# Loads of keys, values and weights in pieces of 1 to 1.5 KB, and a longer hand-written list for the first part

## The chip, the core and the metric

The kernel runs on one core of one Trainium2 chip. A core has a matrix engine (TensorE, PE in the profile, with the weight loads apart as PEld), three engines for elementwise work (VectorE or DVE, ScalarE or ACT, GpSimd or POOL), an engine that issues transfers (SyncE or SP) and 16 DMA engines that move data between the device memory and the on-chip memory. The metric is device time in microseconds, the median of several runs. What is looked at in the profile is one execution.

## What is computed

Four batches of 768 tokens go through three steps, all in fp32:

```python
# 1: attention, 4 x 8 heads of 64, in chunks of 32 tokens: each chunk sees 8 memory keys,
#    16 keys to its left, its own 32 and 8 to its right
scores = scale * q_c @ k_full.T
a = exp(scores - max); a = a / (sum(a) + 1e-09)
x = a @ v_full
# 2: mixing over tokens
theta = x @ w_theta
y = w_tok_r @ (x * cos(theta)) + w_tok_i @ (x * sin(theta))
u = x + y
x = u + relu(u @ w_ch)
# 3: a gated MLP with a token mix
h = gelu(x @ w_in); u, v = halves of h
out = x + (u * (w_sg @ layernorm(v) + b_sg)) @ w_out
```

## The kernel before, in words

**Arithmetic.** Products run on TensorE at reduced precision, so each operand is split into a high and a low part, and three matmuls (high x high, high x low, low x high) stand for one. Weights are split once (`conv_*`, for `w_theta` and `w_tok`), operands as they come (`op_hi` on ACT, `op_lo` on DVE).

**Stages.** The attention goes through 24 blocks of 128 tokens, six for each batch. Behind each block stand theta's matmuls (four steps of three). The token mix of batch 0 runs as plain products between the blocks (`mix_pe`), 48 of them. The token mix of batches 1 to 3 runs as Strassen-Winograd: seven products on half-size operands, each in two halves of 18 matmuls of 128 x 384 (`prod`, L593 to L614, the matmul is L611). For it the weights are combined into s1, s2, s3, a22 (`t_raw`, `t_hi`, `t_lo`, for i = 1 to 4; the combination t3, which makes s3, is used by product 5, and its raw result lies in the room `rin`). x and the fractions of theta of these batches are stored to device memory (`store_xt`, `store_ft`) and loaded again (`in_load`), for batches 2 and 3 into three rooms in `rin`. From them come the operands a11 to a22: sine and cosine on ACT (`zz_sin`, `zz_abs`, `zz_cos`), times x on DVE (`zz_mul`). Then come relu(u @ w_ch) (`chan`) and the MLP, which the change leaves alone.

**What sets the order.** The first part is written out by hand: the string `OPENING` is a list of words, and inside `tc.manual_schedule()` each engine gets its instructions in the list's order, each issued by the function that the table `step` names. Behind the list, from L1104 on, Python code is written in natural order and a scheduler places it. Before, the list ends with `P.1.3.1`, the second half of product 3 of batch 1, and the rest of batch 1 (operand 4, t3, products 4 to 6, the reload for batch 2) is placed by the scheduler.

**Words that the change and the prediction touch.** `q.i`, `k.i`, `v.i`: loads of block i, with two buffers each, on SP's queue as all transfers are. `wt.k`, `wm.j`: loads of pieces of `w_theta` and `w_tok`. `S.i`: scores, 64 small matmuls and their 64 weight loads (`pairs`, L282 to L293, the matmul is L287); `V.i`: probabilities times values, the same shape; `T`, `X`: transposes (L345, L377). `A.i.k`: theta's matmuls (L412); `ac`, `af`: its fraction, on ACT and DVE (L418, L422). `M.n.g`: token mix of batch 0 (L472). `W.n`: n matmuls on the constant tile `busy` whose result nobody reads (L1071); here they are called fillers. `P.b.j.e`: half e of product j of batch b. `ss`, `oh`, `ol`: the sum, high and low part of an operand (L580, L584, L589). `t3`, `t3h`, `t3l`: the steps of t3 (DVE L506 to L509, ACT L515, DVE L518). `cx`, `cy` and, new, `rd`: the reads of finished products, which add a PSUM bank into a sum on DVE (`o_add`, L633); `lr`/`lo` and `sr`/`rs` load and store these sums. `li.b.d.h.j`: the reload (`in_load`, L537), then `ZS`, `ZA`, `ZC`, `ZZ`.

**Layout of the loads.** A block's k is one transfer of 128 rows, each 4096 B in one piece; v has 4160 B a row, `w_theta` 4096 B, `w_tok` 6144 B. x and theta are stored as 2048 B a row, and batch 1 reads them again as three pieces of 1024 B a row, since it takes half of the columns at a time.

Of the kernel before, what the change touches and what calls it, by code (L numbers as in the profile page):

```python
# [19 lines left out]
DM = H * D  # L20
# [14 lines left out]
wt.0 q.0 q.1 wt.1 id.0 wt.3 k.0 k.1 thH.0 v.0 v.1 thR.0 ths.0 wt.2 thg.0 wm.0 wm.1 tha.0 wm.2 thh.0  # L35
thl.0 thH.1 thR.1 ths.1 thg.1 tha.1 thh.1 W.16 S.0 thl.1 q.2 m.0 thH.3 k.2 p.0 thR.3 ths.3 e.0 W.6
S.1 thg.3 k.3 T.0 m.1 q.3 t.0 p.1 tha.3 e.1 W.3 V.0 thh.3 v.2 r.0 T.1 thH.2 x.0 t.1 ths.2 thR.2 X.0
thg.2 w.0 tha.2 h.0 thl.3 thh.2 l.0 tkH.1 thl.2 sT.0 W.8 A.0.0 tkR.1 tks.1 A.0.1 tkg.1 tkH.0 A.0.2
tkR.0 tks.0 tkg.0 S.2 m.2 k.4 A.0.3 q.4 p.2 ac.0 tka.0 e.2 V.1 af.0 tkh.0 v.3 T.2 r.1 wm.3 t.2 x.1
tkl.0 X.1 S.3 tka.1 as.0 w.1 q.5 m.3 wm.4 h.1 k.5 p.3 aa.0 l.1 ak.0 W.5 V.2 z.0 sT.1 A.1.0 v.4 r.2  # L40
x.2 e.3 A.1.1 tkh.1 T.3 tkH.2 tkl.1 S.4 t.3 m.4 q.6 A.1.2 zh.0 k.6 tks.2 tkH.3 X.2 p.4 A.1.3 w.2
tks.3 V.3 h.2 zl.0 ac.1 l.2 v.5 M.0.0 e.4 r.3 sT.2 af.1 tkR.3 T.4 x.3 A.2.0 tkg.2 S.5 tkg.3 as.1 t.4
k.7 A.2.1 aa.1 m.5 lu.5.0 X.3 ak.1 q.7 p.5 tkR.2 A.2.2 z.1 w.3 V.4 tka.3 v.6 A.2.3 r.4 tka.2 M.0.1
e.5 x.4 ac.2 wm.5 T.5 h.3 wm.6 af.2 S.6 t.5 l.3 zh.1 q.8 m.6 X.4 tkh.3 sT.3 A.3.0 p.6 k.8 w.4 M.0.2
tkl.3 h.4 e.6 A.3.1 l.4 tkH.5 zl.1 T.6 sT.4 A.3.2 tkh.2 tks.5 V.5 tkl.2 v.7 A.3.3 r.5 as.2 x.5 t.6
M.1.0 tkg.5 ac.3 aa.2 X.5 af.3 ak.2 S.7 w.5 z.2 as.3 q.9 A.4.0 m.7 zh.2 k.9 tkH.6 M.1.1 zl.2 h.5
tks.6 A.4.1 aa.3 p.7 ak.3 M.1.2 tkg.6 z.3 V.6 l.5 e.7 v.8 A.4.2 tkR.5 r.6 sT.5 x.6 T.7 tkR.6 A.4.3
tka.5 t.7 S.8 tka.6 ac.4 tkh.5 q.10 X.6 m.8 k.10 M.0.3 tkh.6 af.4 sx.6 lu.5.1 p.8 w.6 A.5.0 lu.5.2
zh.3 tkl.5 M.1.3 e.8 zl.3 h.6 V.7 l.6 tkl.6 sT.6 T.8 v.9 as.4 A.5.1 r.7 t.8 x.7 aa.4 A.5.2 ak.4
tkH.4 z.4 S.9 zh.4 q.11 m.9 A.5.3 tkR.4 k.11 X.7 p.9 ac.5 zl.4 sx.7 V.8 w.7 af.5 h.7 v.10 r.8 A.6.0  # L50
# [41 lines left out]
def net_kernel(tc, qt, kw, vw, ident, w_theta, w_tok, w_ch, w_in, w_sg, w_out, g_ln, b_sg, out):  # L92
# [225 lines left out]
    def load_k(i):  # L318
        nc.sync.dma_start(out=ka[i % 2], in_=kw[i])

    def load_v(i):
        nc.sync.dma_start(out=va[i % 2], in_=vw[i])
# [270 lines left out]
    def prod(b, j, e):  # L593
# [4 lines left out]
        if j == 1:  # L598
            bank["y", e] = acc_tile()[:, 0:TC]
# [736 lines left out]
```

## Time and profile before

| what | value |
|---|---|
| median of 3 runs | 752.41 us (752.05 to 753.37) |
| profiled execution | 756.5 us, its span 754.4 us |
| mean granted TensorE clock | 0.977 |
| TensorE busy | 709.2 us (94%) |
| VectorE, ScalarE busy | 533.8 us (71%), 376.3 us (50%) |
| transfers | 59,861 packets, 118.32 MB, mean 157 GB/s |
| chain that ended last | PE 73%, DVE 11%, DMA 7%, issue 4%, ACT 4% |

The profile is of one execution, which took 756.5 us; the runs that are timed have no profile. Times in the trace count from the start of the span. "Busy" adds up the instructions of an engine, where matmuls overlap. "Issue" as what ended a wait means that the engine waited for nothing that the profile shows. The granted clock is a share of full speed. In the trace the opening list goes to about 270 us, `P.1.3.1`; the products of batch 1 end at about 297 us; `chan` and the MLP fill the time from 385 us on.

### The profile page before, as it was taken

To read this page: it belongs to the slowest core of one execution; us is meant where nothing else is said; L and a number is where in the kernel's file an instruction comes from. 1 tells how busy PE (TensorE), PEld (TensorE's weight loads), DVE (VectorE), ACT (ScalarE), POOL (GpSimd) and SP (SyncE) were. 2 spreads that over 40 slices of the span, in tenths; PEclk is the share of its full clock that TensorE was granted. 3 is DMA by queue.
4 is the path that set the end of the run, shared out by engine and by line. 5 is a ranking of instruction groups with operands and counts; after the bars stand their busy time and mean duration, and the time that the engine had idled before them with its cause. 6 is when DMAs were issued, how large, how long until landed. Compare 5 with 4: busy or idle time off the path is not lost.

```text
span 754.4 us, 15661 instructions
## 1 busy us (share of the span) xinstructions
PE 709.2 (94%) x6602; PEld 643.2 (85%) x6602; DVE 533.8 (71%) x851; ACT 376.3 (50%) x551; POOL 0.3 (0%) x6
## 2 busy tenths in 40 slices
PE   6789797999899888999999999999999999999997
PEld 3567575787689878999999998999899989998997
DVE  5888697887684995979749955968346744674375
ACT  4889798688663454553516515812251234223320
POOL 0000000000000000000000000000000000000000
PEclk8899899999999988999999999999999999999999
DMA  9888798899664327333439956001300220030002
GB/s 343 302 305 250 256 340 332 265 318 299 215 197 153 124 76 264 111 105 123 147 85 354 310 186 256 3 1 43 125 1 1 88 80 1 1 111 17 0 1 84
DMA packets 59861, 118.32 MB, mean 157 GB/s; under 512 B 5520, under 2 KB 37392, under 8 KB 59792
## 3 DMA queue, kind: packets, MB, share of 16 engines
q1 hardware_dynamic: 59792, 117.33, 46.0%
q8 instruction: 52, 0.85, 0.5%
q14 instruction: 17, 0.14, 0.1%
HBM read 82.71 MB, written 34.60 MB: 156 GB/s over the span
## 4 chain that ended last, share of the span: by engine, by line
PE 73%; DVE 11%; DMA 7%; issue 4%; ACT 4%; SPq 1%; DVEq 0%; ACTq 0%
PE acc L909 13%; PE acc L694 9%; PE acc L802 7%; PE att L611 7%; PE acc L840 7%; PE th L412 6%; PE att L947 6%; PE acc L611 5%; PE acc L472 4%; PE att L287 4%; DMA right<-ft_dram 3%; DMA xT_dram<-left_o 1%; PE th L611 1%; PE att L345 1%; PE th L947 1%
## 5 line engine op out<-in xcount | busy, mean ns | idle before, releaser
L412 PE MATMUL th<-left 128*128 128x512 f32 x288 | 90.2, 425 | 4.0 <-issue 2.1
L611 PE MATMUL att<-left,at 128*128 128x384 f32 x342 | 67.2, 352 | 7.5 <-DVE left_o L633 4.1
L611 PEld LDWEIGHTS att<-left,at 128*128 128x128 f32 x342 | 62.5, 198 | 10.4 <-DVE left_o L633 4.8
L287 PEld LDWEIGHTS att<-at 64*32 64x32 f32 x3072 | 35.6, 110 | 37.1 <-issue 34.7
L694 PE MATMUL acc<-at,in 128*128 128x384 f32 x384 | 66.9, 335 | 0.0
L694 PEld LDWEIGHTS acc<-at,in 128*128 128x128 f32 x384 | 66.6, 188 | 0.0
L909 PE MATMUL acc<-sg_hi,vhi_all 128*128 128x384 f32 x192 | 64.6, 336 | 0.5 <-ACT vhi_all L209 0.5
L909 PE MATMUL acc<-sg_hi,vlo_all 128*128 128x384 f32 x192 | 64.6, 336 | 0.1
L909 PE MATMUL acc<-sg_lo,vhi_all 128*128 128x384 f32 x192 | 64.5, 336 | 0.0
L287 PE MATMUL att<-at 64*32 64x64 f32 (+1 forms) x3072 | 45.2, 234 | 20.0 <-issue 15.2
L412 PEld LDWEIGHTS th<-left 128*128 128x128 f32 x288 | 50.2, 193 | 13.9 <-DVE in L422 3.2
L472 PE MATMUL acc<-left 128*128 128x384 f32 x288 | 59.5, 342 | 1.1 <-issue 1.1
L209 ACT ACTIVATE gop<-gv_all 128x384 fp32r<-128x384 f32 (+1 forms) x28 | 16.0, 571 | 80.6 <-DVE gv_all L918 53.8
L472 PEld LDWEIGHTS acc<-left 128*128 128x128 f32 x288 | 51.0, 188 | 3.9
L584 ACT ACTIVATE at<-right 128x768 fp32r<-128x768 f32 x42 | 34.9, 842 | 37.7 <-DVE right L580 11.8
L914 DVE SCALAR_TENSOR_TENSOR gv_all<-acc,g_col,b_bc 128x384 f32<-128x384 f32 x32 | 19.7, 616 | 43.1 <-PE acc L909 43.1
L611 PE MATMUL acc<-left,at 128*128 128x384 f32 x252 | 44.9, 337 | 0.0
L611 PEld LDWEIGHTS acc<-left,at 128*128 128x128 f32 x252 | 43.8, 188 | 0.3
L840 PE MATMUL acc<-x3lo,in_hi 128*128 128x384 f32 x128 | 43.1, 337 | 0.0
L840 PE MATMUL acc<-x3hi,in_hi 128*128 128x384 f32 x128 | 43.1, 337 | 0.0
L840 PE MATMUL acc<-x3hi,in_lo 128*128 128x384 f32 x128 | 43.1, 337 | 0.0
L589 DVE TENSOR_TENSOR at<-right,at 128x768 fp32r<-128x768 f32 x42 | 39.4, 954 | 5.1 <-ACT at L584 4.6
(188 smaller groups left out, 1468.6 us busy)
## 6 DMA issues: line engine op xcount, KB each, us to landing
at<-vw SPq DMA_DIRECT2D x24, 520.0 KB, 6.0
at<-kw SPq DMA_DIRECT2D x24, 512.0 KB, 6.2
right<-w_tok SPq DMA_DIRECT2D x12, 768.0 KB, 9.0
at<-qt SPq DMA_DIRECT2D x24, 256.0 KB, 5.0
xT_dram<-left_o SPq DMA_DIRECT2D x24, 256.0 KB, 6.6
left_o<-xT_dram SPq DMA_DIRECT2D x32, 192.0 KB, 2.7
u_dram<-left_o SPq DMA_DIRECT2D x32, 192.0 KB, 1.9
right<-u_dram SPq DMA_DIRECT2D x8, 768.0 KB, 5.9
```

What stands on the lines that cost most here:

```text
L287: nc.tensor.matmul(out=out[32 * c:32 * c + 32, j, n * a:n * a + n], lhsT=lhs[h, a, 32 * c:32 * c + 32], rhs=rhs[h, 4 * a + c, :], start=Tr ...
L412: nc.tensor.matmul(out=tmp["th", i], lhsT=a[:, k], rhs=w[:, k], start=(k == 0 and j == 0), stop=(k == KD - 1 and j == 2),)
L472: nc.tensor.matmul(out=acc_t[g][:, 0:TC], lhsT=z_part(n, a)[:, ri, zc], rhs=w_part(s, h, b)[:, ri], start=(first and i == 0), stop=(last a ...
L584: nc.scalar.activation(out=op_room(b, j)[0][:, s], in_=op_src(j, h), func=AF.Copy)
L589: nc.vector.tensor_tensor(out=lo[:, s], in0=op_src(j, h), in1=r32(hi[:, s]), op=ALU.subtract)
L611: nc.tensor.matmul(out=bank[to, e], lhsT=a[:, s, ee], rhs=w[:, s], start=(fresh and i == 0), stop=(i == 3 * NBLK - 1), skip_group_check=no ...
L694: nc.tensor.matmul(out=acc[:, 0:TC], lhsT=w[:, k, ee], rhs=x[:, k, :], start=(i == 0), stop=(i == 3 * KD - 1),)
L802: nc.tensor.matmul(out=acc, lhsT=x[:, k, tt], rhs=w[:, k, :], start=(i == 0), stop=(i == 3 * KD - 1),)
L840: nc.tensor.matmul(out=acc[:, 0:TC], lhsT=w[:, k, ff], rhs=x[:, k, :], start=(i == 0), stop=(i == 3 * KD - 1),)
L909: nc.tensor.matmul(out=acc[:, 0:TC], lhsT=v, rhs=w, start=(i == 0), stop=(i == 3 * NBLK - 1))
L914: nc.vector.scalar_tensor_tensor(out=g, in0=acc[:, 0:TC], scalar=p3["g"][:, f:f + 1], in1=p3["b"][:, tt], op0=ALU.mult, op1=ALU.add,)
L947: nc.tensor.matmul(out=bank, lhsT=wt[:, k, ee], rhs=xt[:, k, :], start=(fresh and i == 0), stop=(i == 5), skip_group_check=not fresh,)
```

## The change

k, v, `w_theta` and `w_tok` are laid out by the host in four pieces a row, so that a row of 128 comes as 4 x 1024 B (v 4 x 1040, `w_tok` 4 x 1536). x and theta are stored as 2 x 1024 B a row, in place of 2048 B, with which batch 1 reads 3072 B in one piece; batches 2 and 3 read 6144 B as before.

The list is a new one and reaches to `P.2.0.1`, the first product of batch 2. It takes in the rest of batch 1: t3, operands 4 to 6, the loads, reads and stores of the sums, the reload for batch 2. `t3` now stands ahead of the operands 4 and 5, right behind `t4l`. Banks are named by batch as well, as batch 2 begins while reads of batch 1 are out. In the list's first part the order of all words is another, and the fillers are 64 matmuls in place of 38.

```diff
 OPENING = """
-wt.0 q.0 q.1 wt.1 id.0 wt.3 k.0 k.1 thH.0 v.0 v.1 thR.0 ths.0 wt.2 thg.0 wm.0 wm.1 tha.0 wm.2 thh.0
...
-cx.1.1 sr.1.0 t4l.0 oh.1.3.0 P.1.2.0 cy.1.1 ss.1.3.1 sr.1.1 ol.1.3.0 oh.1.3.1 ol.1.3.1 P.1.2.1 t4.1
-P.1.3.0 t4h.1 t4l.1 P.1.3.1
+q.0 wt.0 v.0 k.0 q.1 k.1 id.0 wt.1 wt.2 v.1 wt.3 wm.0 wm.1 thH.0 wm.2 ths.0 thR.0 thg.0 tha.0 thh.0
...
+ss.1.4.0 ac.23 ss.1.4.1 t4h.1 af.23 t4h.0 sf.23 P.1.2.0 t4l.1 t4l.0 lo.1.3.0 t3.0 lo.1.2.0 P.1.2.1
+lo.1.1.0 lo.1.2.1 lo.1.3.1 lo.1.1.1 rd.1.2.0 oh.1.4.0 P.1.3.0 t3.1 t3h.0 oh.1.4.1 P.1.3.1 ol.1.4.0
+t3h.1 ol.1.4.1 t3l.1 P.1.4.0 oh.1.5.0 t3l.0 oh.1.5.1 rd.1.2.1 li.2.0.0.0 ol.1.5.1 li.2.0.1.0
...
+P.2.0.0 rd.1.6.1 rs.1.6.1 P.2.0.1
 """
...
-    xt_dram = [dram.tile([128, 3, DM], F32, name=f"xt_dram{i}") for i in range(2 * B)]
-    ft_dram = [dram.tile([128, 3, DM], F32, name=f"ft_dram{i}") for i in range(2 * B)]
+    xt_dram = [dram.tile([128, 2, 3, 256], F32, name=f"xt_dram{i}") for i in range(2 * B)]
+    ft_dram = [dram.tile([128, 2, 3, 256], F32, name=f"ft_dram{i}") for i in range(2 * B)]
...
     def load_k(i):
-        nc.sync.dma_start(out=ka[i % 2], in_=kw[i])
+        nc.sync.dma_start(
+            out=ka[i % 2].rearrange("p (a c) k -> p a c k", a=NPAIR), in_=kw[i].rearrange("a p c k -> p a c k")
+        )
...
-        nc.sync.dma_start(out=xt_dram[c][:, j], in_=xt_t(i))
+        nc.sync.dma_start(out=xt_dram[c][:, :, j], in_=xt_t(i).rearrange("p (d c) -> p d c", d=2))
...
-            nc.sync.dma_start(out=in_src(b, d, h, j), in_=src[:, :, 256 * d:256 * d + 256])
+            nc.sync.dma_start(out=in_src(b, d, h, j), in_=src[:, d])
...
         def load_th(k):
-            nc.sync.dma_start(out=raw_room("th", k), in_=w_theta[k].bitcast(I32))
+            nc.sync.dma_start(
+                out=raw_room("th", k).rearrange("p (g n) -> p g n", g=4),
+                in_=w_theta[k].bitcast(I32).rearrange("g p n -> p g n"),
+            )
...
-        for b in range(1, B):
-            first = 4 if b == 1 else 0
+        for b in range(2, B):
             for r in QUAD:
                 for e in range(2):
...
-                for j in (2, 3):
-                    for e in range(2):
-                        read(b, j, e)
-                operand(b, 4)
-                t_make(3)
-                z_load(2)
-            for j in range(first, 7):
+                    o_load(b, r, e)
+            if b == 2:
+                for e in range(2):
+                    read(b, 0, e)
+                operand(b, 1)
+            for j in range(1 if b == 2 else 0, 7):
```

The order of the transfers on SP at the program's start, before (`in<-w_theta` is `wt`, `at<-qt`, `at<-kw`, `at<-vw` are `q`, `k`, `v`):

```order
L1005 DMA in<-w_theta 128x1024
L316 DMA at<-qt 128x512 x2
L1005 DMA in<-w_theta 128x1024
L997 DMA id_sb<-ident 128x128
L1005 DMA in<-w_theta 128x1024
L319 DMA at<-kw 128x1024 x2
L322 DMA at<-vw 128x1040 x2
```

and after (the line numbers of the changed kernel are up to 14 higher):

```order
L323 DMA at<-qt 128x512
L1016 DMA in<-w_theta 128x4x256
L331 DMA at<-vw 128x4x260
L326 DMA at<-kw 128x4x256
L323 DMA at<-qt 128x512
L326 DMA at<-kw 128x4x256
L1008 DMA id_sb<-ident 128x128
L1016 DMA in<-w_theta 128x4x256 x2
```

The first v and k now stand third and fourth, where the first k was seventh, and three of the four pieces of `w_theta` come behind them.

On DVE, in the stretch of products 3 to 5 of batch 1, before (L633 reads, L589 is `ol`, L506, L507, L509 are the steps of `t3`, L518 with `left<-in` is `t3l`):

```order
L589 TENSOR_TENSOR at<-right,at 128x768
L518 TENSOR_TENSOR left<-in,left 128x1152
L506 TENSOR_TENSOR in<-left 128x1152
L589 TENSOR_TENSOR at<-right,at 128x768
L507 TENSOR_TENSOR in<-in,left 128x1152
L589 TENSOR_TENSOR at<-right,at 128x768
L509 TENSOR_TENSOR in<-in,left 128x1152
L633 TENSOR_TENSOR left_o<-th,left_o 128x384
L633 TENSOR_TENSOR left_o<-att,left_o 128x384
L589 TENSOR_TENSOR at<-right,at 128x768
L518 TENSOR_TENSOR left<-in,left 128x1152
```

and after, behind `af.23` (L529 is L518 of before, L517, L518, L520 are the steps of `t3`, L600 is `ol`, L644 reads; L228 and L231 split a piece of `w_ch`):

```order
L529 TENSOR_TENSOR left<-left_o,left 128x1152 x2
L517 TENSOR_TENSOR in<-left 128x1152
L228 SCALAR_TENSOR_TENSOR left_o<-left_o 128x256
L518 TENSOR_TENSOR in<-in,left 128x1152
L231 ISA left_o<-left_o 128x512
L520 TENSOR_TENSOR in<-in,left 128x1152
L644 TENSOR_TENSOR left_o<-th,left_o 128x384
L517 TENSOR_TENSOR in<-left 128x1152
L518 TENSOR_TENSOR in<-in,left 128x1152
L520 TENSOR_TENSOR in<-in,left 128x1152
L600 TENSOR_TENSOR at<-right,at 128x768 x2
L529 TENSOR_TENSOR left<-in,left 128x1152 x2
```

The six raw steps of `t3` now stand together, with one read and two steps of `w_ch` between them, and the operand's low parts and the reads have moved behind or to other places.

## Rows read from the trace of the kernel before

**Rows 1.** The page's busy table: engine, busy us, share of span, instructions.

```profile
PE 709.2 (94%) x6602; PEld 643.2 (85%) x6602; DVE 533.8 (71%) x851; ACT 376.3 (50%) x551; POOL 0.3 (0%) x6
```

**Rows 2.** Windows, us: PE, PEld, DVE, ACT, POOL busy; granted clock, DMA share, GB/s.

```profile
0.00:254.00 254.00, 222.84 (x3950) 176.72 (x3950) 193.11 (x301) 182.50 (x271) 0.33 (x6) 0.95 0.80 268
254.00:298.00 44.00, 36.80 (x183) 34.94 (x184) 33.98 (x40) 22.43 (x26) 0.00 (x0) 0.88 0.48 160
298.00:385.00 87.00, 84.84 (x487) 83.94 (x486) 72.56 (x106) 40.59 (x60) 0.00 (x0) 1.00 0.37 121
385.00:754.00 369.00, 364.72 (x1986) 347.59 (x1984) 234.17 (x407) 130.82 (x194) 0.00 (x0) 1.00 0.26 88
280.00:290.00 10.00, 8.54 (x26) 7.72 (x26) 2.14 (x4) 4.81 (x7) 0.00 (x0) 0.55 0.79 275
```

**Rows 3.** PE's waits, 0 to 254 us: us in total, times, longest.

```profile
PE att L287 <- issue: 15.2, 11, 2.6
PE att L287 <- DMA at<-kw: 3.9, 1, 3.9
PE att L377 <- ACT at L351: 2.5, 3, 1.1
PE th L412 <- issue: 2.1, 2, 1.6
```

**Rows 4.** PE's timeline at the start: start, us, line, count, wait ahead.

```profile
1.05 5.88 PE L1071 MATMUL acc<-busy 128*128 128x512 bf16 x16 [1.05 <-DVE busy L994]
10.84 1.17 PE L287 MATMUL att<-at 64*32 64x64 f32 x64 [3.91 <-DMA at<-kw]
```

**Rows 5.** PE's timeline, products of batch 1 to the first of batch 2.

```profile
255.87 3.40 PE L611 MATMUL th<-b,at 128*128 128x384 f32 x18 [1.92 <-DVE in L422]
...
279.06 0.69 PE L611 MATMUL att<-left,at 128*128 128x384 f32 x1 [2.62 <-ACT left L515]
...
284.08 5.62 PE L611 MATMUL att<-left,at 128*128 128x384 f32 x18 [0.65 <-DVE left_o L633]
...
297.62 2.59 PE L611 MATMUL acc<-left,at 128*128 128x384 f32 x14
```

**Rows 6.** The chain that ended last, products of batch 2 (start, us).

```profile
329.06 12.48 PE acc L611 x72
```

**Rows 7.** Windows of 8 to 23 and 155 to 175 us, columns as above.

```profile
8.00:23.00 15.00, 9.73 (x221) 5.68 (x222) 10.37 (x20) 8.51 (x15) 0.00 (x0) 0.77 1.03 412
155.00:175.00 20.00, 18.90 (x396) 15.15 (x395) 14.85 (x22) 17.67 (x26) 0.00 (x0) 1.00 1.01 334
```

**Rows 8.** SP's timeline at the start.

```profile
3.55 1.11 SPq L319 DMA_DIRECT2D at<-kw  x2
```

**Rows 9.** DMA, 0 to 254 us by slices; packets of 8:23, of 155:175.

```profile
DMA  6999699699588779999867999999767949075360
...
DMA packets 1545, 6.18 MB, mean 412 GB/s; under 512 B 174, under 2 KB 174, under 8 KB 1544
...
DMA packets 4860, 6.68 MB, mean 334 GB/s; under 512 B 312, under 2 KB 3375, under 8 KB 4857
```

**Rows 10.** PE's timeline at 88 us.

```profile
88.26 0.66 PE L287 MATMUL att<-at 64*32 64x64 f32 x26 [2.44 <-issue]
```

**Rows 11.** The page's DMA queues: packets, MB, share of 16 engines.

```profile
q8 instruction: 52, 0.85, 0.5%
```

**Rows 12.** DVE's timeline, 277 to 280 us.

```profile
277.29 0.56 DVE L633 TENSOR_TENSOR left_o<-th,left_o 128x384 f32<-128x384 f32 x1
...
278.22 0.96 DVE L589 TENSOR_TENSOR at<-right,at 128x768 fp32r<-128x768 f32 x1
279.08 1.36 DVE L518 TENSOR_TENSOR left<-in,left 128x1152 fp32r<-128x1152 f32 x1
```

**Rows 13.** SP's timeline at 280 us.

```profile
280.51 0.32 SPq L537 DMA_DIRECT2D in<-ft_dram  x1
```

**Rows 14.** The page's DMA issues: count, KB each, us to landing.

```profile
at<-kw SPq DMA_DIRECT2D x24, 512.0 KB, 6.2
```

More of the change, by code (lines that the diff above doesn't have):

```diff
@@ L40 @@
[L40 to L50, printed above, removed]
@@ L400, in store_xt @@
         c, j = half(i)
-        nc.sync.dma_start(out=xt_dram[c][:, j], in_=xt_t(i))
+        nc.sync.dma_start(out=xt_dram[c][:, :, j], in_=xt_t(i).rearrange("p (d c) -> p d c", d=2))
     def store_ft(i):
         c, j = half(i)
-        nc.sync.dma_start(out=ft_dram[c][:, j], in_=ft_t(i))
+        nc.sync.dma_start(out=ft_dram[c][:, :, j], in_=ft_t(i).rearrange("p (d c) -> p d c", d=2))
     def th_pe(i, k):
@@ L611, in prod @@
                 nc.tensor.matmul(
-                    out=bank[to, e], lhsT=a[:, s, ee], rhs=w[:, s],
+                    out=bank[b, to, e], lhsT=a[:, s, ee], rhs=w[:, s],
                     start=(fresh and i == 0), stop=(i == 3 * NBLK - 1), skip_group_check=not fresh,
@@ L632, in o_add @@
         t = o_room(b, r, e)
-        nc.vector.tensor_tensor(out=t, in0=bank[z, e], in1=t, op=ALU.add)
+        nc.vector.tensor_tensor(out=t, in0=bank[b, z, e], in1=t, op=ALU.add)
     def o_store(b, r, e):
@@ L1004, in load_th @@
         def load_th(k):
-            nc.sync.dma_start(out=raw_room("th", k), in_=w_theta[k].bitcast(I32))
+            nc.sync.dma_start(
+                out=raw_room("th", k).rearrange("p (g n) -> p g n", g=4),
+                in_=w_theta[k].bitcast(I32).rearrange("g p n -> p g n"),
+            )
         def load_tok(j):
-            nc.sync.dma_start(out=raw_room("tk", j), in_=w_tok[j // 2, j % 2].bitcast(I32))
+            nc.sync.dma_start(
+                out=raw_room("tk", j).rearrange("p (g n) -> p g n", g=4),
+                in_=w_tok[j // 2, j % 2].bitcast(I32).rearrange("g p n -> p g n"),
+            )
         def conv_tile(w, j, i):
@@ L1088, in net_kernel @@
             "cy": lambda b, e: o_add(b, "r11", e, "y"), "sr": lambda b, e: o_store(b, "r11", e),
+            "lo": lambda b, r, e: o_load(b, list(QUAD)[r], e),
+            "rd": lambda b, j, e: o_add(b, READS[j][0][0], e, READS[j][0][1]),
+            "rs": lambda b, j, e: o_store(b, READS[j][0][0], e),
         }
-        for i in (1, 2, 4):
+        for i in (1, 2, 3, 4):
             for n, f in (("", t_raw), ("h", t_hi), ("l", t_lo)):
@@ L1109, in operand @@
                 op_lo(b, j, h)
-        def t_make(i):
-            for h in range(2):
-                t_raw(i, h)
-                t_hi(i, h)
-                t_lo(i, h)
         def z_make(b):
@@ L1303, in _layout @@
         "ident": np.eye(128, dtype=np.float32),
-        "w_theta": pieces(inp["moe_w_theta"], DM)[:, 0],
-        "w_tok": pieces(w_tok.reshape(S, 4 * TC), 2 * TC),
+        "w_theta": quarters(pieces(inp["moe_w_theta"], DM)[:, 0]),
+        "w_tok": quarters(pieces(w_tok.reshape(S, 4 * TC), 2 * TC)),
         "w_ch": pieces(inp["moe_w_ch"], 256),
```

122 lines of the change are left out of this document (69 added, 53 removed).

## The prediction

> **What bounds the kernel now.** I read the page's busy table first: TensorE (PE) works 94% of the span [rows 1]. Whatever makes the kernel faster must therefore shorten PE's idle time, or its time at the lower clock. The windows by stage say where these lie [rows 2]: 0 to 254 us (the opening, to the end of product P.1.1.1) has 222.84 of 254.00 busy, 31.2 idle; 254 to 298 (the rest of batch 1's products, the reload for batch 2) has 36.80 of 44.00, 7.2 idle; 298 to 385 has 2.2 idle and 385 to 754 has 4.3. The last two are not touched by the change. So the reader looks at two stages of four.
>
> In the opening, PE's waits [rows 3] name the reasons: 15.2 us in 11 waits in L287 (the small matmuls of S and V) where nothing that the profile shows was awaited ("issue"), 2.1 of the same kind in L412, 3.9 in one wait for k; the rest are sums of 2.5 and less. Issue makes 17.3 us of the 31.2. The wait for k is at the head of the program: the first 16 fillers end, and S.0 starts 3.91 later, at 10.84 [rows 4].
>
> In the tail, from P.1.2.0's start at 255.87 to P.2.0.0's at 297.62 [rows 5], PE does ten products of 18 matmuls in 41.75 us. At the full clock 72 such matmuls take 12.48 [rows 6], 3.12 a product, so ten need 31.2: 10.5 us are lost there. The gap of 2.62 before 279.06 starts it, and the granted clock from 280 to 290 is 0.55 [rows 2], near the lower of PE's two levels (1.2 against 2.4 GHz).
>
> **The change, part by part.**
>
> *Head.* In the old SP order four half-megabyte loads stand ahead of k.0: two of w_theta, q.0 with q.1, a third of w_theta; with the 64 KB of ident and k.0 itself 2624 KB have to move. In the new order q.0, one w_theta, v.0 and k.0 are 256 + 512 + 520 + 512 = 1800 KB. From 8 to 23 us the engines moved 412 GB/s [rows 7]; 824 KB less at that rate is 2.0 us. The k issue stood at 3.55 in SP [rows 8], after six others; now three are ahead, so some tenths more. I take **-2.5**, with bounds -1 (the conversion of w_theta for A.0, whose other pieces now come later, takes part of it back) and -3.5 (the whole wait of 3.9, less what the smaller pieces cost).
>
> *Fillers.* W matmuls go from 38 to 64, 26 more. The first row of 16 took 5.88 us, 0.37 each [rows 4]; by the 0.173 of a 384 column matmul at the full clock [rows 6] one of 512 columns costs 0.23. So 26 are 6.0 to 9.6 us of PE. Of these most stand before A.0, V.1 and S.3, where PE waited anyway (0 to 35 us, where clock and waits are poor). I take **+1**; bounds 0 and +8 (hardly any of it in idle time).
>
> *Pieces.* k and v rows of 4 KB become four pieces of 1 KB: 24 loads x 128 rows x 3 extra, twice, is 18,432 packets; w_tok adds 12 x 128 x 3 = 4608, w_theta 1536, the 36 stores of x and theta 128 each = 4608, batch 1's reloads take 2048 away: 27,136 more packets. What is a packet's own price? From 8 to 23 us 1545 packets took the 16 engines 15 us x 1.03 [rows 7, 9], 160 ns each at 4.0 KB; from 155 to 175 us 4860 took 20 x 1.01, 66.5 ns at 1.37 KB. A straight line through both has 17.6 ns for each packet, and that is an upper end, since the second stretch writes to HBM too while the first only reads. 27,136 x 17.6 / 16 = 30 us of engine time at most, 0 at least (if the difference is the writes'). The opening's DMA share is 0.80 [rows 2], and 19 of its 40 slices stand at 9 [rows 9]; yet of PE's waits of the opening only that for k at the start is a DMA's [rows 3]: the loads are issued a block or more ahead, and that covers it. I take **+1**, bounds 0 and +15 (half of the 30, the half that falls into full slices).
>
> The Trainium skill ("DMA: Bandwidth & Descriptors", section "Why small descriptors are slow (HBM only)") puts a fixed cost of about 3 cycles on a packet, beside one for each 32 bytes. By it four pieces of 1 KB take 140 cycles where one of 4 KB takes 131, 7% more, an estimate from that page that speaks against the change but mildly; the rows above, taken as they stand, would be harder on it (28% more), and no run here yet shows the two sizes for the same load.
>
> *The new order in the opening.* It does the same S, V, A, M work in another order; PE's sum is the same, and dependences are met in a similar way (token-mix products M stand earlier, their weights' loads wm.5 to wm.11 too). What it does to the issue waits is the open question. They fall inside rows of S and V: the typical one is a stop of 2.44 us in the middle of such a row [rows 10]. Instructions come by a DMA queue of their own, 52 packets of 16 KB in the execution [rows 11]; PE has 13,323 instructions, 256 to a packet if all are its own. The waits are as if a block had come late where 64 weight loads and 64 matmuls run off in under a microsecond. The new program has as many PE instructions (61 more), and its S and V rows meet block ends about as often. I take **0**, bounds -9 (half of the 17.3) and +4.
>
> The Trainium skill ("Runtime: NRT & Kernel Launch", section "Instruction fetch mechanics") tells of blocks of 256 instructions that are fetched ahead and says that this is hidden by the rate of issue. The trace disagrees: there are 15.2 us of issue waits in L287. If the page were right these waits would belong to the order and could vanish with a new one, which is the third rival below.
>
> *Tail.* Before, DVE works through operand 4, t3's first raw step and operand 5, then t3l of the second half ends at 280.44 [rows 12]; only then may the reload li.2 overwrite t3's room (issue at 280.51 [rows 13]); theta's fractions and x arrive, their sine, cosine and product make the operand, and P.2.0.0 starts at 297.62, 17.2 us after t3l. PE meanwhile waits 2.62 for t3h, falls to the lower clock, and is slowed for P.1.5 and P.1.6. After the change DVE does t3 at once: from P.1.2.0's start on, 2 t4l and 6 t3 steps and 2 t3l are 10 x 1.36, 2 operand steps 2 x 0.96, a read 0.56, two small w_ch steps under 0.96 each (1.9): 18.0 us [rows 12]. PE needs 6 x 3.12 = 18.7 for P.1.2 to P.1.4, so s3 is there when P.1.5 asks, with 0.7 to spare: no 2.62, no fall of the clock. Next late is the reload: it starts 18.0 after P.1.2.0 and, with the same 17.2, gives P.2.0.0 at 35.2, while PE is done with all ten products at 31.2 plus two reads' bubbles of 0.65 [rows 5] = 32.5. So PE waits 2.7 for it, and the stretch takes 35.2 in place of 41.75: **-6.5**. Bounds: -10 (reload in PE's shadow) and -2 (4.5 us lost to the operand steps that now mix with the reload's on ACT and DVE). The wait for af.23 ahead of P.1.2.0 (1.92 before) stays: A.23 now stands behind P.1.1.1, and DVE has about as much ahead of af.23.
>
> *Rest.* The later reads of batch 1 (rd, rs) move before the first product of batch 2; stage 298 to 385 has 2.2 us of PE idle in all [rows 2], so nothing is counted for it: 0, with the bounds 0 and +1.
>
> **The sum.** -2.5 + 1 + 1 + 0 - 6.5 = -7. The profiled execution took 756.5 us, with a span of 754.4; it would be 749.5. The median of the runs is 752.41, 4.1 under it, and gives 745.
>
> **Rivals.**
> 1. *The tail isn't paid.* The chain to P.2.0.0 (t3l, reload, sine, product with x, split) is what ends last after the change, and it could keep its old end: ACT takes the operand steps oh.1.5 and oh.1.6 between the sines, and the second half's reload waits for the sines of the first. For it: the chain already is the later one by my sum. Against: DVE frees t3's room about 6.5 us earlier against PE's work (280.44 - 255.87 = 24.6, then 18.0). Tail 0, the rest of the sum -0.5: 752.
> 2. *Slower: the DMA engines become the bound of the opening.* Place: the loads of k and v, two buffers each, with wm.5 to wm.11 now issued earlier between them. Price: 17.6 ns a packet, 30 us of engine time, half of it in slices that are already full: +15 in place of +1, so 745 + 14 = 759. It decides from the point at which a k or v load lands later than the block before it is done, a lead of one block, 10.6 us (24 blocks in 254 us), against 6.2 us from issue to landing [rows 14]. For it: the share of 0.80 would rise to 0.9 or so. Against: no wait for k or v after the start now.
> 3. *The issue waits shrink.* If they come from instruction blocks that queue behind data packets of 4 KB, pieces of 1 KB let them through sooner; or the old order makes them, and the new one has them elsewhere, shorter. Half of 17.3 gone is 9 more: 736, between 731 and 740. For it: a stop of 2.44 is far longer than 16 KB need on one of the 16 engines at 412 GB/s for all (0.64 us, an estimate from [rows 7]). Against: no row ties a stop to the size of the packets around it, and the ends of the blocks stay as many. By the rule of the Trainium skill's page ("Runtime: NRT & Kernel Launch", the section above) the order would make all of them.
>
> **How the numbers follow.** The forecast (740 to 750) has 0.56, the unpaid tail 0.12, the DMA bound 0.15, the shrunk issue waits 0.17. Measured against 752.4, 0.2% (1.5 us) is about what a measurement of this kernel can tell from no change: the first and the last are faster, 0.73; the unpaid tail is the same, 0.12; slower 0.15. The range reaches from the third rival's middle, less the tail's better bound, 733, to just over the unpaid tail, 754, and leaves out the DMA bound and an end of the third rival.
>
> **What would show it.** Head: S.0 in PE's timeline at about 8.3 in place of 10.84. Tail: P.1.2.0 to P.2.0.0 in about 35 us, no wait for left at P.1.5.0, the granted clock 1.00 until the wait before P.2.0.0. Pieces: no PE waits for at<-kw or at<-vw past the first block; the DMA share of the opening at 0.82 to 0.9. Issue: the waits in L287 between 13 and 17 us. Wrong it would be if the opening up to P.1.2.0 came out over 5 us longer or shorter than now by waits for k and v, or by a change of the issue waits, or if the reload moved with PE's products and not with t3.

## The result and the profile after

The changed kernel took 742.8 us, the median of four runs (740.69 to 744.91), beside 752.89 for the kernel before; the ratio is 0.9864, with the interval 0.9825 to 0.9903. Nine later runs gave 743.66 against 752.81, ratio 0.9899 (0.9863 to 0.9935). So the change is worth some 7.6 to 10.2 us. The forecast was 745, in the range 733 to 754.

The profiled execution took 741.19 us, its span 739.3. Its busy table and its stages, cut at P.1.2.0, P.2.0.0 and two later points, with the columns of [rows 2] ([rows 2] is cut at 254 and 298, where P.1.2.0 came at 255.87 and P.2.0.0 at 297.62):

```profile
PE 704.5 (95%) x6628; PEld 638.7 (86%) x6628; DVE 531.2 (72%) x851; ACT 371.7 (50%) x551; POOL 0.3 (0%) x6
```

```profile
0.00:247.00 247.00, 220.97 (x3976) 174.03 (x3976) 195.79 (x309) 180.38 (x273) 0.33 (x6) 0.99 0.86 273
247.00:281.80 34.80, 33.40 (x180) 32.79 (x181) 28.80 (x31) 19.55 (x24) 0.00 (x0) 0.95 0.59 194
281.80:370.00 88.20, 84.97 (x484) 83.28 (x483) 72.34 (x107) 41.19 (x62) 0.00 (x0) 1.00 0.40 130
370.00:739.00 369.00, 365.19 (x1992) 348.61 (x1990) 234.27 (x407) 130.56 (x194) 0.00 (x0) 1.00 0.26 88
```

The opening has 26.0 us of PE idle where it had 31.2 (33.0 up to P.1.2.0), and its clock is 0.99 where it was 0.95; the DMA share rose from 0.80 to 0.86. The tail is 34.8 long. The later stages are as they were.

PE's waits over the whole program (us in total, times, longest), which answer to [rows 3], and its timeline at the start, which answers to [rows 4]:

```profile
PE att L294 <- issue: 7.3, 7, 2.0
...
PE att L294 <- DMA at<-kw: 3.5, 1, 3.5
PE att L356 <- issue: 3.2, 1, 3.2
...
PE acc L483 <- issue: 0.6, 1, 0.6
PE acc L1088 <- issue: 0.5, 1, 0.5
```

```profile
1.05 5.46 PE L1088 MATMUL acc<-busy 128*128 128x512 bf16 x16 [1.05 <-DVE busy L1005]
10.03 0.85 PE L294 MATMUL att<-at 64*32 64x64 f32 x64 [3.53 <-DMA at<-kw]
...
25.22 3.27 PE L423 MATMUL th<-left 128*128 128x512 f32 x12
```

L294 is L287 of before. Issue waits are 11.6 us in all, with 18.4 before: 15.2 and 2.1 from [rows 3], and 1.1 in a row for L472. S.0 starts at 10.03 (10.84 before), but the first theta product A.0 only at 25.22 (23.02 before).

The tail in PE's timeline, which answers to [rows 5]:

```profile
247.01 4.97 PE L622 MATMUL th<-b,at 128*128 128x384 f32 x18 [1.99 <-DVE in L433]
...
264.29 9.53 PE L622 MATMUL att<-left,at 128*128 128x384 f32 x54
274.56 3.38 PE L622 MATMUL att<-left,at 128*128 128x384 f32 x18 [0.74 <-DVE left_o L644]
...
281.82 0.51 PE L622 MATMUL acc<-left,at 128*128 128x384 f32 x2
282.79 1.85 PE L622 MATMUL acc<-left,at 128*128 128x384 f32 x9 [0.45 <-DVE at L600]
...
295.69 3.28 PE L622 MATMUL th<-b,at 128*128 128x384 f32 x18
```

No wait for t3 stands ahead of product 5 (it is inside the row of 54 matmuls at 264.29), and P.2.0.0 comes 34.81 after P.1.2.0, where it was 41.75. It has waits of 0.45 and 0.35 for its operand. P.1.2.0 itself, behind the wait of 1.99, took 4.97 us where it took 3.40 before [rows 5]; the granted clock of 247 to 252 us is 0.66.

**One execution is not the kernel.** The profiled execution of before, 756.5 us, was at the upper end of its runs. A second one of each kernel was therefore looked at, and these two lie near the medians of their kernels.

> The kernel before once more, unchanged, for a second profiled execution. The first took 756.5 us, the upper end of its runs (747.6 to 760.9 in the later ones), so its 18.4 us of issue waits may be more than usual. Theory (the places of the block ends set the issue waits, executions scatter by 2 to 3 us): 15 to 20 us of issue waits. Rival (the scatter is as large as the differences between the kernels): 10 to 13 us, as in the changed kernel.

> The changed kernel once more, unchanged, beside the next two on one chip. Theory (the change is worth 1.2 to 1.5%): ratio 0.985 to 0.988, issue waits of its profiled execution 8 to 13 us, P.1.2.0 to P.2.2.0 within 0.3 us of 48.7. Rival (the first four runs were lucky): ratio over 0.99.

They took 750.45 and 742.5 us. Waits of the first, then of the second:

```profile
PE att L287 <- issue: 11.5, 10, 2.2
...
PE acc L472 <- issue: 1.4, 1, 1.4
...
PE th L412 <- issue: 0.6, 1, 0.6
```

```profile
PE att L294 <- issue: 8.0, 7, 1.9
...
PE acc L483 <- issue: 0.2, 1, 0.2
```

That is 13.5 us before, under the 15 to 20 that was expected, and 8.2 after, as expected. The ratio of the second round, 0.9899, missed the expected 0.985 to 0.988 and came out just under the rival's 0.99. Between these two executions the difference goes as follows, by events in PE's timeline. P.2.2.0 is a better end of the tail than P.2.0.0, since work of batch 2 can stand between batch 1's products.

| stretch | before (748.4 span) | after (740.6 span) | difference |
|---|---|---|---|
| start to A.0 | 23.45 | 26.62 | +3.2 |
| A.0 to P.1.2.0 | 227.13 | 222.27 | -4.9 |
| P.1.2.0 to P.2.2.0 | 54.22 | 48.67 | -5.6 |
| P.2.2.0 to the end | 443.6 | 443.0 | -0.6 |

### The profile page after: what moved, and what is told of

It reads as the page before. It is cut to its first block, busy times and chain, and to the rows that moved or that the text cites. A ratio compares the mean times of both kernels' runs of the same rounds, so it can differ in the third digit from the quotient of the medians.

```text
span 739.3 us, 15734 instructions
## 1 busy us (share of the span) xinstructions
PE 704.5 (95%) x6628; PEld 638.7 (86%) x6628; DVE 531.2 (72%) x851; ACT 371.7 (50%) x551; POOL 0.3 (0%) x6
## 3 DMA queue, kind: packets, MB, share of 16 engines
q1 hardware_dynamic: 86928, 117.33, 48.5%
## 4 chain that ended last, share of the span: by engine, by line
PE 70%; DVE 12%; DMA 7%; ACT 7%; issue 4%; SPq 1%; DVEq 0%; ACTq 0%
PE acc L920 14%; PE acc L813 9%; PE acc L851 9%; PE acc L705 9%; PE att L622 6%; PE att L958 6%; PE th L423 3%; PE acc L622 3%; PE att L294 2%; PE th L622 2%; PE acc L483 2%; DMA right<-xt_dram 2%; DVE at L600 1%; DVE right L565 1%; PE th L958 1%
## 5 line engine op out<-in xcount | busy, mean ns | idle before, releaser
L423 PE MATMUL th<-left 128*128 128x512 f32 x288 | 86.9, 414 | 1.8 <-DVE in L433 1.5
L622 PE MATMUL att<-left,at 128*128 128x384 f32 x342 | 62.4, 338 | 3.8 <-DVE left_o L644 3.8
L622 PEld LDWEIGHTS att<-left,at 128*128 128x128 f32 x342 | 59.2, 188 | 5.8 <-DVE left_o L644 3.3
L294 PEld LDWEIGHTS att<-at 64*32 64x32 f32 x3072 | 34.3, 105 | 30.7 <-issue 25.3
L294 PE MATMUL att<-at 64*32 64x64 f32 (+1 forms) x3072 | 42.7, 224 | 13.4 <-issue 7.3
L600 DVE TENSOR_TENSOR at<-right,at 128x768 fp32r<-128x768 f32 x42 | 39.4, 953 | 9.5 <-ACT at L595 9.2
```

Source lines behind the costliest of these rows:

```text
L294: nc.tensor.matmul(out=out[32 * c:32 * c + 32, j, n * a:n * a + n], lhsT=lhs[h, a, 32 * c:32 * c + 32], rhs=rhs[h, 4 * a + c, :], start=Tr ...
L423: nc.tensor.matmul(out=tmp["th", i], lhsT=a[:, k], rhs=w[:, k], start=(k == 0 and j == 0), stop=(k == KD - 1 and j == 2),)
L600: nc.vector.tensor_tensor(out=lo[:, s], in0=op_src(j, h), in1=r32(hi[:, s]), op=ALU.subtract)
L622: nc.tensor.matmul(out=bank[b, to, e], lhsT=a[:, s, ee], rhs=w[:, s], start=(fresh and i == 0), stop=(i == 3 * NBLK - 1), skip_group_check ...
```

## The experiments

They were run in three rounds, and each ratio is to runs of the kernel before in the same round. The medians of these were 753.71 us (transfers alone, whole rows, the first cut list, the shift by 64), 751.19 (the shifts by 160 and 32, small fillers, the second cut list) and 752.81 (k and v in pieces, the shift by 80, the changed kernel again), so between rounds the ratios are to be compared and not the times.

### Which part makes the gain: transfers or list

The first kernel has the list and the code of before, and only the transfers of the change.

```diff
 # the kernel before
-        nc.sync.dma_start(out=ka[i % 2], in_=kw[i])
+        nc.sync.dma_start(out=ka[i % 2].rearrange(...), in_=kw[i].rearrange("a p c k -> p a c k"))
... v, w_theta, w_tok, x and theta likewise
```

> The kernel before with the changed transfers alone (k, v, w_theta, w_tok in four pieces a row, x and theta stored in two); the list and TensorE's instructions are those of before. Theory (the pieces cost a little DMA time and nothing else; the issue waits hang on where TensorE's blocks of instructions end, and those ends are where they were): opening's DMA share up from 0.80 to about 0.83 to 0.86, issue waits of TensorE still 16 to 20 us, time 752 to 755. Rival (smaller packets let the instruction blocks through sooner): issue waits at 12 us or less as in the changed kernel, time 743 to 748.

It took 755.74 us, just over the expected range, ratio 1.0033 (1.0002 to 1.0065): slower by 0.02 to 0.65%. Its issue waits are 17.7 us in all, in about the number and size of before, so smaller packets don't let the instruction blocks through sooner. The DMA rate falls where the loads fill the engines. The stretch of 8 to 23 us, its window and its packets, of this kernel (before: [rows 7, 9]):

```profile
8.00:23.00 15.00, 7.92 (x212) 4.82 (x213) 9.44 (x18) 7.17 (x12) 0.00 (x0) 0.86 1.08 363
```

```profile
DMA packets 4573, 5.44 MB, mean 363 GB/s; under 512 B 147, under 2 KB 4479, under 8 KB 4572
```

363 GB/s where the whole rows gave 412, in the same stretch with the same loads, at a full share. The profiled executions of all kernels agree on this: 410 to 413 GB/s in the seven with whole rows, 360 to 363 in the six with all the pieces, 391 in the one with k and v alone in pieces. In this kernel S.0 starts at 11.74 and A.0 at 25.90, 0.9 and 2.9 later than in the kernel before.

The second kernel is the other half: the new list, with whole rows.

```diff
 # the changed kernel
-        nc.sync.dma_start(out=ka[i % 2].rearrange(...), in_=kw[i].rearrange("a p c k -> p a c k"))
+        nc.sync.dma_start(out=ka[i % 2], in_=kw[i])
... v, w_theta, w_tok, x and theta likewise
```

> The new list and the code behind it, with the transfers of before (whole rows of 4 and 6 KB). Theory (the list makes the gain): issue waits as in the changed kernel, 9 to 14 us, P.1.2.0 to P.2.0.0 about 35 us, time 740 to 745. Rival (the pieces make the opening's gain): issue waits back at about 18 us, time 749 to 752, of the gain only the tail's 7 us left at most.

It took 737.89 us, ratio 0.9807 (0.9767 to 0.9847), the fastest of all and faster than the 740 to 745 expected. The list makes the gain; the pieces take a part of it away (the changed kernel's interval, 0.9825 to 0.9903 in the first runs, overlaps with this one by a little, that of the later runs does not). PE's timeline at the start and its issue waits:

```profile
9.08 1.05 PE L294 MATMUL att<-at 64*32 64x64 f32 x64 [2.02 <-DMA at<-kw]
...
22.88 3.42 PE L419 MATMUL th<-left 128*128 128x512 f32 x12
```

```profile
PE att L294 <- issue: 6.9, 8, 2.0
...
PE att L294 <- DMA at<-kw: 2.0, 1, 2.0
```

S.0 at 9.08 is what the new SP order gives, 1.8 us; in the changed kernel it starts 0.9 later (10.03). A.0 stands at 22.88, where it stood before, and in the changed kernel 2.3 to 3.7 later. Over all profiled executions with the new list A.0 starts at 21.48 to 22.94 in the three with whole rows and at 23.56 to 26.62 in the five with all the pieces. At S.0 the two groups are not as clear: 8.97 to 9.08, and 8.60 to 10.03.

To see which pieces cost, k and v alone were taken in pieces, in the kernel with the new list and whole rows.

> The new list with whole-row transfers (ratio 0.981 to the kernel before), in which k and v alone come in pieces of 1 KB; weights and stores stay whole. Theory (the pieces' price is DMA time before the first theta product A.0, in proportion to their packets; k and v are 18,432 of the 27,136, but of the 3.9 MB ahead of A.0 only 2 MB): S.0 at 9.6 to 10.1 against 9.08, A.0 at 23.5 to 24.5 against 22.9, ratio 0.983 to 0.986. Rival (the price lies in the weights' pieces, which A.0 waits for): ratio 0.979 to 0.982, A.0 within 0.3 us of 22.9.

It took 742.66 us, ratio 0.9879 (0.9832 to 0.9926), slower than either side had expected by the middle of the ratios. Its timeline at the start:

```profile
8.44 0.85 PE L294 MATMUL att<-at 64*32 64x64 f32 x64 [1.88 <-DMA at<-kw]
...
23.48 3.11 PE L423 MATMUL th<-left 128*128 128x512 f32 x12
```

S.0 started before the 9.08 of whole rows, where 9.6 to 10.1 was expected, and A.0 0.6 later than with whole rows, so by this one execution most of the delay of A.0 comes from the pieces of the weights, against the theory's share. Yet the time is that of all the pieces, and what it lost lies spread behind A.0 (224.5 us to P.1.2.0 against 220.4). Its interval holds both ratios of the changed kernel and overlaps with that of whole rows, so where the pieces of k and v cost is not settled.

### Why the issue waits fell

The idea under test: an issue wait comes where a block of instructions ends inside work that runs off fast. The ends were read from the instruction order (13,323 instructions over the 52 packets of [rows 11], and the places of the stops in the trace). For each of the 31 ends in the opening a count took the time in which the 64 instructions ahead of it run off, by durations of the trace (S and V 128 in 0.86 us, a weight load with its matmul 0.17 to 0.21), and summed what is missing to 2.5 us, about the longest stop. The 64 and the 2.5 are assumptions, made after the result and before the runs. The sum is 34 us for the kernel before and 27 for the changed one; over all 256 places that the ends could take it goes from 26 to 36 for the second. By this count the new list has nearly its best place. That the old list had one of its worst, as the expectations below say, hangs on the durations that the count takes: by the starts of the matmuls in the traces the new list again has nearly its best place (31 to 32 us, of 31 to 39), but the old one a middling one (35 to 36, of 31 to 38).

The ends can be seen in the traces themselves. Number PE's instructions in order (weight loads, matmuls and semaphore instructions). In the 14 profiled executions PE stops 147 times for over 0.15 us with "issue" as the reason, 161 us in all. 107 of these stops, 126 us, come at instruction 192 to 195 behind a multiple of 256. Before, that is 15.7 of the 18.4 us and 10.5 of the 13.5 in the second execution; after, 9.2 of 11.6 and 5.1 of 8.2. So the fall of the issue waits lies in the stops at block ends. The largest of the others, 1.2 to 2.0 us ahead of V.1, is in 13 of the 14 executions and moves with the instructions put in ahead of it, so it belongs to that place of the list. Why a block comes late at one end and not at another is not settled by it.

The test puts small matmuls behind the first 16 fillers, in the wait for k. They cost 0.03 us each and shift every later block end.

```diff
+        def tiny(n):
+            bank = acc_tile()
+            for _ in range(n):
+                nc.tensor.matmul(out=bank[0:32, 0:32], lhsT=busy[:, 0:32], rhs=busy[:, 0:32], start=True, stop=True)
...
-... W.16 S.0 ...
+... W.16 N.32 S.0 ...
```

> The kernel before with 32 matmuls of 32 columns (64 instructions of TensorE) more behind the first 16 fillers, where TensorE waits 3.9 us for k anyway; nothing else is changed. Theory (the issue waits come where a block of 256 instructions ends inside S or V, whose 128 instructions run off in 0.86 us; 64 instructions ahead, the block ends meet other work): issue waits fall by 4 to 8 us from 18.4, time 745 to 750. Rival (the waits hang on the load on the DMA engines, or on the list's order, not on where blocks end): issue waits 16 to 20 us, time 752 to 754.

747.07 us, ratio 0.9920 (0.9890 to 0.9950), by 64 instructions that compute nothing; the theory's ranges held. Waits:

```profile
PE att L287 <- issue: 10.7, 12, 3.2
...
PE th L412 <- issue: 0.2, 1, 0.2
```

Beside the second execution of before the fall is 2.6 us, and A.0 comes 1.6 us earlier, with a granted clock of 0.95 in the first 35 us (0.82 and 0.84 in the two executions of before). So a part of the gain can be the start's clock, which this run does not separate.

> The kernel before with 80 matmuls of 32 columns (160 instructions, about 2.4 us) more behind the first 16 fillers, in the wait for k; nothing else is changed. By the same count of block ends the summed shortage is 27.5 us, against 34 before and 28 with 64 instructions more, which measured 747.1 against 753.7. Theory (places of the block ends): issue waits 9 to 13 us, time 745 to 749. Rival (64 instructions more were faster for the higher clock that the 32 matmuls gave the start, not for the places; 80 matmuls give that as well but the issue waits don't follow the count): issue waits 15 us or more, time 750 to 754.

753.91 us, ratio 1.0030 (0.9996 to 1.0063). The issue waits did fall, to 12.8, but the time did not:

```profile
PE att L287 <- issue: 12.4, 10, 2.3
...
PE att L345 <- ACT at L339: 2.7, 1, 2.7
...
PE acc L472 <- issue: 0.4, 1, 0.4
```

S.0 started 0.9 later than in the first execution of before, and a wait for ACT is 2.7 (1.5 in the second execution of before); the granted clock of the first 35 us is 0.88. Beside the second execution of before, with 13.5 us of issue waits and 750.45 us, the fall is only 0.7. The time forecast of the theory failed here; why the waits fell by less and the time not at all stays open.

> The changed kernel with 16 matmuls of 32 columns (32 instructions of TensorE, 0.03 us each) more behind the first 16 fillers, in the 3.5 us in which TensorE waits for k; nothing else is changed. Counting, along the instruction order, how fast the 64 instructions ahead of each block's end run off (a block is 256 instructions, its end falls at 193 plus a multiple of 256; S and V run off 64 in 0.43 us, products in over 5), the changed kernel has one of the best places of the 256 (summed shortage 27 us by this count, where it goes from 26 to 36), the kernel before one of the worst (34); 32 instructions on it is 35. Theory (the places of the block ends set the issue waits): issue waits up by 4 to 8 us from 11.6, time 746 to 751. Rival (the new list has fewer issue waits for another reason): 10 to 13 us, time 741 to 745.

746.87 us, ratio 0.9926 (0.9897 to 0.9956); the changed kernel is at 0.9864 and 0.9899, and this interval overlaps with those of both, with the first by very little. The issue waits rose to 15.5, though S.0 started 1.4 us earlier:

```profile
PE att L294 <- issue: 13.3, 11, 3.2
...
PE th L423 <- issue: 2.2, 2, 1.2
```

> The new list with whole-row transfers and 40 matmuls of 32 columns (80 instructions, about 1.2 us) more behind the first 16 fillers, in the 2.0 us in which TensorE waits for k. By the count of block ends the summed shortage goes from 27 to 34 us. Theory (places of the block ends): issue waits from 6.9 to 11 or more, ratio 0.987 to 0.993 against 0.981. Rival (160 instructions more in the kernel before left its time where it was against this count; the count says nothing): issue waits 5 to 8 us, ratio 0.980 to 0.983.

742.48 us, ratio 0.9886 (0.9835 to 0.9937), against 0.9807 without the shift; the two intervals overlap by a little:

```profile
PE att L294 <- issue: 14.0, 11, 2.8
```

All profiled executions together, sorted by the count:

| count, us | kernels | issue waits, us |
|---|---|---|
| 27 to 28 | changed, twice | 11.6, 8.2 |
| 27 to 28 | changed with the list cut, twice | 8.1, 11.6 |
| 27 to 28 | new list, whole rows; with k, v in pieces; with tiny fillers | 6.9; 7.7; 4.6 |
| 27 to 28 | before, shifted by 64; by 160 | 10.9; 12.8 |
| 34 to 35 | before, twice | 18.4, 13.5 |
| 34 to 35 | before with pieces | 17.7 |
| 34 to 35 | changed, shifted by 32; whole rows, shifted by 80 | 15.5; 14.0 |

The most in the first group, 12.8, is less than the least in the second, 13.5; the means are 9.2 and 15.8. So the places of the block ends do set a good part of the issue waits, as the stops' own places in the instruction order show too. They do not set all of the time: one shift of four did not show in it, executions of one kernel differ by 3 to 5 us in these waits, and of the changed kernel's two the one with more of them was the faster (741.2 with 11.6, 742.5 with 8.2; its granted clock was 0.995 in place of 0.985). The count itself is no model of their size (27 where 5 to 13 are waited).

### The fillers

In the kernel with the new list and whole rows the 48 fillers behind the first 16 became matmuls of 32 columns, the same in number.

```diff
-S.0 m.0 q.2 k.2 p.0 e.0 W.5 S.1 ... W.4 V.0 ... W.8
+S.0 m.0 q.2 k.2 p.0 e.0 N.5 S.1 ... N.4 V.0 ... N.8
... W.10, W.7, W.7, W.5, W.2 likewise
```

> The new list with whole-row transfers (737.9 in the first runs), in which the 48 fillers behind the first 16 are matmuls of 32 columns, the same number of instructions but 0.03 us each in place of 0.2 to 0.4; the places of the block ends stay. Theory (the fillers stand in time in which TensorE waits for the first blocks and keep the granted clock up): time 738 to 743, the clock in 0 to 35 us lower than the 0.95 of it. Rival (they lie on the path, some 10 us of them): time 728 to 735.

740.37 us, ratio 0.9849 (0.9815 to 0.9883), against 0.9807 with them: no faster, by the middle of the ratios 3 us slower, with intervals that overlap. The window of the first 35 us shows what they do, this kernel first, the one with fillers second:

```profile
0.00:35.00 35.00, 21.68 (x405) 13.97 (x405) 23.58 (x40) 21.44 (x31) 0.33 (x6) 0.72 0.90 343
```

```profile
0.00:35.00 35.00, 27.15 (x471) 14.53 (x472) 23.60 (x41) 22.36 (x33) 0.33 (x6) 0.95 0.94 355
```

Without them PE is busy 5.5 us less and the granted clock is 0.72 against 0.95 (0.85 to 1.00 in the seven other executions of the new list, all with fillers). A.0 starts at 22.9 in both. The fillers lie in time that PE waits anyway.

### The tail

The changed kernel's list was cut behind P.1.3.1, and the rest of batch 1 left to the scheduler, as before.

```diff
-... sf.23 P.1.2.0 t4l.1 t4l.0 lo.1.3.0 t3.0 lo.1.2.0 P.1.2.1 ... P.2.0.1
+... sf.23 P.1.2.0 t4l.1 t4l.0 P.1.2.1 P.1.3.0 P.1.3.1
-        for b in range(2, B):
+        for b in range(1, B):
+            first = 4 if b == 1 else 0
... ss.1.4 leaves the list, the code behind the list is that of before
```

> The changed kernel with its list cut behind P.1.3.1 and the rest of batch 1 (operand 4, t3, products 4 to 6, the reload for batch 2) placed by the scheduler as before; the opening and the transfers are the changed kernel's. Theory (the tail gives about 7 us by itself): P.1.2.0 to P.2.0.0 back at 40 to 43 us against 34.8, a wait of 2 to 3 us for t3 ahead of product 5 and a granted clock near 0.55 behind it, time 749 to 751. Rival (the shorter tail is given back later, or the scheduler does as well behind the new opening): time 742 to 745.

744.68 us, ratio 0.9896 (0.9856 to 0.9936). In this kernel the operand sum of product 5 (`ss.1.5`) was made twice, by the list and by the code, which adds two DVE steps and changes the operand, so this kernel computes something else and serves for its times alone. It was run again with that sum made once:

> The cut list again (the changed kernel with the rest of batch 1 behind P.1.3.1 placed by the scheduler), now with the operand sum of product 5 made once, by the scheduled code; in the first such run it was made twice, and that run gave 744.7 with the tail's products at 249.9 to 288.6 and matmuls of batch 2 between them. Theory (the new opening alone lets the scheduler reach a tail nearly as short, since t4 and the sums of the operands are done earlier; the longer list gives 1 to 3 us): time 743 to 746. Rival (the double sum hid or made the difference; the list's tail gives its 7 us): 748 to 751.

745.96 us, ratio 0.9925 (0.9894 to 0.9955). The theory of the first of these two runs, that the tail gives 7 us by itself, failed: the times are those of its rival, and the second run's theory, 743 to 746, held. Against the two ratios of the changed kernel the long list is worth 2 to 5 us, though the intervals overlap. But not where I had put it. The tail in PE's timeline, the cut list first, the changed kernel's start and end of the same 14 products second (247.01 and 295.69, shown above):

```profile
249.65 4.61 PE L415 MATMUL th<-left 128*128 128x512 f32 x12 [3.71 <-DVE in L425]
255.66 3.39 PE L614 MATMUL th<-b,at 128*128 128x384 f32 x18 [1.41 <-DVE in L425]
...
282.92 0.96 PE L614 MATMUL acc<-left,at 128*128 128x384 f32 x4 [1.09 <-ACT at L587]
...
303.05 3.28 PE L614 MATMUL th<-b,at 128*128 128x384 f32 x18
```

47.39 us from P.1.2.0 to P.2.2.0, no longer than the 48.68 of the long list, and far under the 54.3 of before. Its P.1.2.0 took 3.39 us, so it lacks the slow 4.97 of the changed kernel. There is no wait for t3: behind the new opening, which has made t4 and the operand sums by then, the scheduler puts t3 as early as the list does, and the reload with it, so that matmuls of batch 2 (`acc<-`, at 282.92) fill in between. What the long list saves lies ahead: here A.23 waits 3.71 for a DVE step that stands behind others, and 0.88 in the changed kernel.

## Why the prediction came out as it did

The time, 745, lies 1 to 2 us over the measured 743, and the range held. The sum was right in total by terms that were wrong in opposite ways, and that is luck: of the large terms only the tail was foreseen.

**Tail, -6.5: right in size.** Measured -6.9 to P.2.0.0 and -5.6 to P.2.2.0. DVE's order freed t3 in time, the wait of 2.62 and the half clock behind it went, and the next late thing was the operand of batch 2. The clock did not stay at 1.00 as forecast: it fell behind the wait for af.23, ahead of P.1.2.0, and cost 1.6 us there (4.97 against 3.40). The chain from t3l to P.2.0.0 was estimated to cost PE 2.7 us; it cost 0.8 (waits of 0.45 and 0.35). What I took as the cause, the place of t3 in the list, is only the nearest one: the cut list gives as short a tail. The work that the new opening does before P.1.2.0 is the cause that the runs bear out; a kernel with the old opening and the new tail was not tried.

**Head, -2.5: wrong.** The order of the loads gives 1.8 to S.0 (9.08 with whole rows), near the 2.0 that the bytes gave. Two steps failed behind that. The pieces, which I had costed elsewhere, take a part of it at the start (0.9 at S.0 in the profiled execution, though S.0 with pieces scatters from 8.60 to 10.03). And S.0 is not what the head is for: A.0, the first large work, starts no earlier with whole rows (22.88 against 23.02) and 2.2 to 3.2 later with pieces. The bound "-1, since the conversion of w_theta takes part of it back" named the mechanism and did not go far enough.

**Pieces, +1: too small, inside the bounds.** Measured +2.5 us with the old list (0.33%), and 4 to 7 with the new one (0.9807 to 0.9864 and 0.9899). The engine time of 0 to 30 us came out at 8 to 12: the queue's share of the span went from 46.0% of 754.4 to 47.2% of 752.8 and 48.5% of 739.3, which is 5 to 7 ns for each of the 27,136 packets, where the line through [rows 7, 9] gave 17.6. (The 28% that the prediction takes from this line is a slip: three more packets of 17.6 ns on 160 are 33%. Nothing in the sum hangs on it.) The queue's rows of the page, of the kernel before, with the transfers alone, and of the changed kernel:

```profile
q1 hardware_dynamic: 59792, 117.33, 46.0%
```

```profile
q1 hardware_dynamic: 86928, 117.33, 47.2%
```

```profile
q1 hardware_dynamic: 86928, 117.33, 48.5%
```

The mistake was to look for the exposure in the waits for k and v in mid-opening. A part of it lies at the start, where all loads come at 363 GB/s in place of 412 and A.0 is later (23.56 to 26.62 with all the pieces, 21.48 to 22.94 without); with k and v alone in pieces A.0 was 0.6 later and the time still that of all the pieces, so where the rest is paid stays open. The page's estimate from the Trainium skill ("DMA: Bandwidth & Descriptors", section "Why small descriptors are slow (HBM only)") of 7% on these loads is of the right order: an estimate by it is 6 us (7% of the 90 us that the 36 MB of k, v and weights take at 412 GB/s), and 8 to 12 are measured over these and the stores. In 8 to 23 us, where the loads fill the engines, it is more: the same bytes took 13% longer (363 against 412 GB/s).

**Issue waits, 0: wrong, the largest error.** The sentence "its S and V rows meet block ends about as often" held: 23 of the 31 ends in the opening lie in such rows in both kernels. The step that failed is the one from there to 0. As many ends do not make as many stops: 12 ends stopped PE before and 9 in the second execution, 8 and 4 after. The count lays this to how much of the fast work stands ahead of each end. The waits fell from 18.4 and 13.5 to 11.6 and 8.2, 5 to 7 us, and the stops' places in the instruction order and the shifts show that the block ends have the main part in it. Nothing in the change aims at these places, so this gain is luck as well. By the prediction's own sign of being wrong (the opening over 5 us shorter by a change of the issue waits) the first two executions call it wrong (P.1.2.0 at 255.87, then 247.01), the second two do not (250.58, then 248.89), as there the 3.2 us by which A.0 came later take back most of the 4.9 behind it. The third rival said that these waits shrink, with a chance of 0.17; its reason by small packets is refuted by the old list with pieces (17.7), its other reason, the list, is what happened. Its time, 731 to 740, came only with whole rows (737.9). The Trainium skill ("Runtime: NRT & Kernel Launch", section "Instruction fetch mechanics") calls the fetch of instruction blocks mostly hidden; every trace here disagrees, with 2 to 16 us of stops at the ends of blocks of 256, and 64 idle instructions at the start changed the time by 0.8%.

**Fillers, +1: about nothing or a gain.** No cost shows (ratio 0.9849 with small matmuls in their place, 0.9807 with them). The bound of +8 was not needed: A.0 started at 22.9 either way.

**The DMA rival** (759) did not come: the share rose to 0.86, and the only wait of PE for a DMA is the one for the first k.

In numbers between the two executions near the medians: +3.2 to A.0 (forecast -2.5 with +1 for pieces and +1 for fillers), -4.9 from there to P.1.2.0 (forecast 0), -5.6 (forecast -6.5).

## What to carry to other kernels

When a list is replaced, small stops that nothing explains can move with it; number the engine's instructions and see whether the stops come at one place modulo 256. A few empty instructions at the start, in a wait that is there anyway, test it; as these waits scatter by 3 to 5 us between executions, more than one run is needed, and one shift of four here changed no time. Measure the parts of a change apart: here the list alone (ratio 0.981) is better than list and pieces (0.986 and 0.990). Follow a gain at the head to the first work that is really long, and take a second profile before reading single waits of 2 us as the kernel's.

## What the runs showed of the hardware

- 107 of 147 stops of TensorE for no reason that the profile shows (126 of 161 us, 14 executions) came at instruction 192 to 195 behind a multiple of 256.
- 64 instructions of TensorE that compute nothing (32 matmuls of 0.03 us) changed 753.7 us to 747.1, and 160 left it where it was (ratio 1.003); 32 of them in the changed kernel cost it 2 to 5 us by the middles of the ratios.
- The same loads at a full share of the DMA engines moved 410 to 413 GB/s in rows of 4 KB and more, and 360 to 363 GB/s in rows of 1 to 1.5 KB.
- Executions of the same kernel differ by 3.4 to 4.9 us in issue waits (18.4 and 13.5 before; 11.6 and 8.2 after), and in the granted clock of the first 35 us (0.82 and 0.84; 0.95 and 0.85).
- Without the fillers the granted clock of the first 35 us was 0.72, with them 0.95, and A.0 came at the same time.
